# A two-layer-pair transformer on one core: GpSimd fill and mask work taken out of layer 0, ones rows written in small loads, a new planner model

## The chip, the cores and the metric

The kernel runs on one core of one Trainium2 chip. Its engines each work through an instruction list of their own: TensorE (PE) multiplies matrices, VectorE (DVE) and ScalarE (ACT) do elementwise work and empty PSUM, GpSimd (POOL) does small set-up work, and SyncE (SP) and ACT issue DMAs. The metric is the device time of one execution in microseconds. The kernel before took 397.16 us, the median of four runs (394.88 to 398.32 us).

## The reference

Four residual layers are run over 2048 tokens of width 448, in bfloat16: attention (A), gated MLP (B), A, B, with the same weights both times. A query sees eight keys, at distances 0, 2, ..., 14, inside its own head.

```python
def _A_ref(x, wqkv, wo):
    B, S, D = x.shape
    H = 16; Dh = D // H
    W, dil = 8, 2
    ...
    idx = pos[:, None] - off[None, :]
    mask = idx >= 0
    ...
    logits = jnp.einsum("bhsd,bhswd->bhsw", q, kg) * scale
    logits = jnp.where(mask[None, None, :, :], logits, -1e9)
    attn = _softmax(logits, axis=-1)
    o = jnp.einsum("bhsw,bhswd->bhsd", attn, vg)
    return (lambda x, *d: x.transpose(*d))(o, 0, 2, 1, 3).reshape(B, S, D) @ wo

def _B_ref(x, w_gate, w_up, w_down):
    g = jnp.einsum("bsd,df->bsf", x, w_gate)
    u = jnp.einsum("bsd,df->bsf", x, w_up)
    h = g * u
    return jnp.einsum("bsf,fd->bsd", h, w_down)

x = A_x
x = x + _A_ref(_layernorm(x, axis=-1), A_wqkv, A_wo)
x = x + _B_ref(_layernorm(x, axis=-1), B_w_gate, B_w_up, B_w_down)
x = x + _A_ref(_layernorm(x, axis=-1), A_wqkv, A_wo)
x = x + _B_ref(_layernorm(x, axis=-1), B_w_gate, B_w_up, B_w_down)
```

The inputs named `B_x` are not used by the result.

## The kernel before, in words

Even and odd tokens are kept apart (the first 1024 columns are the even ones), so that a dilated window becomes a plain window of eight neighbours. Layers are numbered 0 to 3: 0 and 2 are attention, 1 and 3 the MLP. Each layer is cut into chunks of 256 or 512 tokens; a job "A03" is chunk 3 of layer 0. `SEQ` (L70) lists the jobs in order, and layers overlap: B10 is already listed before A03.

An attention chunk does this. DVE and ACT make the layer norm of each block of 128 tokens (L614 to L635, the last writes `xn_sb`); the block is transposed, in layer 0 by PE through `ident` (L644) and copied from PSUM (L650), in the later layers by a DMA transpose (L638). PE projects Q and K (`qk_chunk`, matmuls at L682), ACT or DVE copies them to `qk` (L734). PE projects V (L682 also), copied to `v_sb` (L823). Attention goes by groups of two query blocks of 120 queries: the scores, 64 small matmuls with 28 rows each ("S", L843); the exponential on ACT into `E_sb` (L850); the band mask, a multiplication by `MK` (L860); the product with V, 64 small matmuls ("AV", L877); then a normalisation on ACT and DVE (L891 to L918) and the output projection (L698).

The last four heads' V is computed along with K and Q, as extra columns. It goes by DMA from `qk` to a scratch tensor `vt` in DRAM ("PW", L743), seven DMAs a chunk, and is read back by a DMA transpose ("VT", L754). `vt` also needs rows of ones, which give the softmax sum: GpSimd fills 16 partitions of 2048 elements (`big1`, L570), and two DMAs on SP write them to the scratch tensors of the two attention layers (L573). The first three query blocks of layer 0 have no such detour (`PLAIN`).

An MLP chunk does 14 units of 14 matmuls (gate and up, L964), a copy of the gate from PSUM on ACT (L970), a product on DVE into `hT` (L973), and the down projection (L698, the last two blocks at L985). `hT` also serves as staging space at the start, for the attention weights, for the mask's parts and for `big1`, so the first writes of L973 wait for the DMAs that read it (L972).

At the start SP issues the x loads, two of the four attention weight loads, then the others; ACT issues the other two weight loads (L501), loads its function table (L509) and issues the two gate loads later (L580). Weights are spread into `WQK` on ACT, DVE or POOL (L557, L565). PE runs 48 matmuls on zeros until real work comes (L548).

The order of all this is not written by hand. A planner (`Sched`) holds every operation with an estimated time, dependencies and a priority, and plays the engines forward: an engine that is free takes the ready operation with the lowest priority number. The resulting order of each engine is what is emitted; on the chip each engine keeps it and waits on semaphores. Estimates and priorities therefore change the order and nothing else. `PR` holds priority offsets by kind of operation, `JP` by job, `HEAD_P` of the first layer norms; `XL`, `STL`, `WVL`, `BL` are assumed landing times of loads; `HOLD_A`, `HOLD_BA`, `HOLD_BB` say how long PE leaves small-matmul work waiting before it turns to it (at once when `HOLD_N`, two, are ready); `A_CAP` and `B_CAP` say how many of the eight PSUM banks attention and MLP work may hold while the other wants some. An S operation takes four banks, a QK or AV operation two. An S or AV group costs PE, in the plan, what `S_EST` says:

```python
S_EST = 270.0
...
by_pool = hp == 1 and li == 0 and (end - 1) // 512 < POOL_MASK
sc.add(("dve", "pool") if by_pool else "dve", ins, {"dve": dve_est(2 * w, 2.0, 60.0 * len(ins)), "pool": 2.2 * 2 * w},
...
big1 = hT[0:4 * VT, 6:8, :, :].rearrange("p f s n -> p (f s n)")
sc.add("pool", one(lambda E: E.memset(big1, 1.0), "c_big1"), 1800, prio=-20)
for li in (0, 2):
    dst = vt_dram[li].rearrange("(t r) n -> t r n", r=32)[:, DH:32, :]
    plain_dma("sp", dst, big1, ("vones", li), f"d_one{li}", deps=["c_big1"], lat=3000.0, prio=-10)
```

Of the kernel before, what the change touches and what calls it, by code (L numbers as in the profile page):

```python
# [9 lines left out]
S = 2048  # L10
D = 448
H = 16
DH = 28
# [6 lines left out]
NQB = 17  # L20
EW = 4 * 128
NGR = 9
SCALE = DH ** -0.5
# [6 lines left out]
HEAD_LN = 5  # L30
HEAD_P = (-32.07, -27.33, -20.7, -18.17, -14.17)
HOLD_A = 1000.0
HOLD_BA = 2000.0
HOLD_BB = 4000.0
HOLD_N = 2
S_EST = 270.0
DPARTS = ((0, 7), (7, 14))
S_AFTER = 9
POOL_MASK = 1
POOL_WQK = True  # L40
VFIRST = False
VT = 4
NV2 = 6
NXN_ = 6
NO = 4
NE_ = 2
# [3 lines left out]
NBK = 8  # L50
PR = {'AV': -1.13, 'rstd': -5.13, 'bn': -0.38, 'N': -4.34, 'Gps': -1.22, 'Tps': 9.06, 'H': 3.83, 'S': -5.56, 'VT': -3.59, 'Ex': 3.61, 'G': 7.67, 'xn': -0.19, 'QK': 2.33, 'Ddps': -11.05, 'V': 10.89, 'x': -0.46, 'lnv': -20.66, 'Oc': -5.93, 'Oa': 1.35, 'R': -8.64, 'VVps': 0.18, 'Yps': 0.16, 'PW': 28.27, 'T': -2.43, 'mv': 0.81, 'Rs': -0.7, 'Rl': 4.01, 'QKps': -0.61, 'E': 0.37}
JP = {'A20': -35.49, 'B32': 2.91, 'B34': 8.11, 'A22': -3.18, 'B13': 0.51, 'A21': 3.14, 'B12': 0.41, 'A02': 0.27, 'A03': 0.46, 'B30': 0.78, 'B31': 0.62, 'B10': -17.75, 'B11': 0.16, 'A23': 11.17, 'A04': 3.65, 'B33': 3.74, 'A01': -0.38, 'B14': -0.22, 'A00': -8.79}
XL = (3000.0, 3000.0, 4500.0, 5000.0, 5500.0)
WVL = 5000.0
STL = (3300.0, 4300.0, 3500.0, 4600.0)
BL = (11000.0, 15000.0, 8000.0)
KP = ((0, 3), (3, 7))
KT = (13000.0, 13500.0)
WOL = 6000.0
PLAIN = 3  # L60
ACH = {0: (256, 512, 512, 512, 256), 2: (512, 512, 512, 512)}
BCH = {1: (256, 512, 512, 512, 256), 3: (256, 512, 512, 512, 256)}
WARM = 18
FILL = 30
SEED = 375
JITTER = 0
ATT_P = 0.44
A_CAP = 8
B_CAP = 8
# [27 lines left out]
def grp_qbs(g):  # L97
    return [0] if g == 0 else [2 * g - 1, 2 * g]

# [25 lines left out]
class Sched:  # L125
# [5 lines left out]
    TAIL = {"pe": 0.0, "act": 125.0, "dve": 85.0, "pool": 100.0, "sp": 0.0}  # L131
    SWITCH = 92.0

    def __init__(self):
# [75 lines left out]
    def schedule(self):  # L210
# [4 lines left out]
        order = {e: [] for e in self.ENGS}  # L215
        mode = None
        ndep, users = {}, {}
        pend = {e: [] for e in self.ENGS}
# [19 lines left out]
        while left:  # L238
            moved = False
            b_ready = any(o.acquire is not None and o.acquire.kind == 1 for o in pend["pe"])  # L240
            for e in self.ENGS:
# [64 lines left out]
                if e == "pe":  # L306
                    if mode is not None and op.mode != mode:
                        est += self.SWITCH
                    mode = op.mode
                op.start, op.end = now, now + est  # L310
                free[e] = op.end
# [111 lines left out]
def build(nc, A_x, A_wqkv, A_wo, B_w_gate, B_w_up, B_w_down, out):  # L423
# [28 lines left out]
    v2_sb = sb([128, NV2, 128], bf, "v2_sb")  # L452
    E_sb = sb([128, NE, 4, EW], bf, "E_sb")
    R_sb = sb([128, NR, EW], dt.float32, "R_sb")
# [20 lines left out]
    def one(fn, key=None):  # L475
        return [(fn, key)]
# [30 lines left out]
    for q in range(2, NCH):  # L507
        load_x(q)
    sc.add("act", one(act_table_load), 1300.0, prio=-58)  # L509

# [9 lines left out]
    sc.add("pool", one(lambda E: E.memset(v_sb[:].rearrange("p s (h e) -> p (s h) e", e=32)[:, :, DH:32], 1.0), "c_v"), 400, prio=-40)  # L520
    sc.add("pool", one(lambda E: E.memset(v2_sb[:, 0:PLAIN, :].rearrange("p s (h e) -> p (s h) e", e=32)[:, :, DH:32], 1.0), "c_v2"), 200, prio=-39)
    memset("pool", MT, 1.0, "i_mt", 300)
# [45 lines left out]
    WVR = [("wv", 0), ("wv", 1)]  # L568
    big1 = hT[0:4 * VT, 6:8, :, :].rearrange("p f s n -> p (f s n)")
    sc.add("pool", one(lambda E: E.memset(big1, 1.0), "c_big1"), 1800, prio=-20)  # L570
    for li in (0, 2):
        dst = vt_dram[li].rearrange("(t r) n -> t r n", r=32)[:, DH:32, :]
        plain_dma("sp", dst, big1, ("vones", li), f"d_one{li}", deps=["c_big1"], lat=3000.0, prio=-10)  # L573
    for j in range(4):
# [10 lines left out]

    rings = {n: [None] * k for n, k in (("xn", NXN), ("o", NO), ("v", NV), ("v2", NV2), ("e", NE), ("r", NR), ("g", NG))}
    rpos = {n: 0 for n in rings}
# [16 lines left out]
    def ln_chunk(li, j, prio):  # L604
# [17 lines left out]
        for B in blocks:  # L622
# [14 lines left out]
            if not by_pe:  # L637
                sc.add("sp", one(lambda E, slot=slot, c0=c0: E.dma_start_transpose(X[:, :, c0:c0 + 128], xn_sb[:, slot, 0:128 * nt]), ("T", li, B)),  # L638
                       1300.0, deps=[("xn", li, B)] + war, dma=f"d_t{li}_{j}", mode=0, lat=2400.0 if li == 0 else 1400.0 if par == 0 else 1900.0, prio=prio)
            else:  # L640
# [61 lines left out]
    def qk_chunk(li, j, prio):  # L702
# [37 lines left out]
        for b, w in [(b, w) for b in range(4) for w in range(2) if b + w < 4 and (li, j) != (0, 0)]:  # L740
            src = qk[32 * b + DH:32 * b + 32, w, :, c0:c1]
            dst = vt_dram[li].rearrange("(t w b r) n -> r w b t n", w=2, b=4, r=4)[:, w, b, :, c0:c1]
            sc.add("sp", one(lambda E, dst=dst, src=src: E.dma_start(dst, src), ("PW", li, j) if b == 3 else None), 550.0, deps=[("QK", li, j, c) for c in range(4)], dma=f"d_p{li}_{j}", mode=0, lat=3000.0 if li == 0 and j <= 2 else 2200.0, prio=prio - 0.2)  # L743

    vslot, v2slot = {}, {}

    def vt_load(li, qb, prio):
        if li == 0 and qb < PLAIN:
            return
        k0, nk, _, _ = qb_info(qb)  # L750
        slot, prev = ring("v2", ("AV", li, qb))
        v2slot[(li, qb)] = slot
        deps = [("PW", li, j) for j in chunks_of(li, k0, k0 + nk)] + [("vones", li), prev]
        sc.add("sp", one(lambda E: E.dma_start_transpose(v2_sb[:, slot, :], vt_dram[li][:, k0:k0 + 128]), ("VT", li, qb)), 1300.0, deps=deps, dma=f"d_v{qb}", mode=li, lat=2000.0 if li == 0 and k0 < 1024 else 1500.0, prio=prio)  # L754

    def v_group(li, qbs, prio):
# [14 lines left out]
        tdeps = [("T", li, B) for B in sorted(blocks)] + [p for _, p in slots if p is not None]  # L771
        plain = li == 0 and qbs[0] < PLAIN
        split = len(qbs) == 1
# [170 lines left out]
    def b_chunk(li, j, n_b, prio):  # L944
# [15 lines left out]
        for m in range(FC):  # L960
# [6 lines left out]
            for u in us[m:m + 1]:  # L967
                bk, fc = u["bk"], u["fc"]
                gs, prev = ring("g", ("H", li, j, fc))
                sc.add("act", one(lambda E, gs=gs, bk=bk: E.activation(g_sb[:, gs, 0:nt], ps[:, bk[0], 0:nt], ACT.Copy), ("G", li, j, fc)), act_est(nt),  # L970
                       deps=[("Gps", li, j, fc), prev], release=[(bk, 0)], prio=prio)
                war = hslot_users.get((hs, "prev"), WQKR + [("vones", 0), ("vones", 2)] + [f"c_mk{k}" for k in range(3)])  # L972
                sc.add("dve", one(lambda E, gs=gs, bk=bk, fc=fc: E.tensor_tensor(hT[:, fc, hs, 0:nt], g_sb[:, gs, 0:nt], ps[:, bk[1], 0:nt], ALU.mult), ("H", li, j, fc)), dve_est(nt),  # L973
                       deps=[("G", li, j, fc), ("Ups", li, j, fc)] + war, release=[(bk, 1)], prio=prio)
# [29 lines left out]
    def grps_of(li, j):  # L1004
        a, z = CH[li][j]
        return [g for g in range(NGR) if a < sum(qb_info(grp_qbs(g)[-1])[2:]) <= z]

    done = {}

    def a_chunk(li, j, prio):  # L1010
# [14 lines left out]

        for g in grps_of(li, j):
            qbs = grp_qbs(g)
            while len(qbs) == 2 and (rpos["v"] % NV) == NV - 1:
# [86 lines left out]
```

## Time and profile before

| | us |
|---|---|
| median of 4 runs | 397.16 |
| lowest, highest | 394.88, 398.32 |
| the profiled execution, its own time | 398.32 |
| its span, first to last instruction | 396.6 |
| DVE busy | 278.6 (70%) |
| ACT busy | 199.6 (50%) |
| POOL busy | 10.2 (3%) |

So 1.7 us of the profiled execution lie outside its span, and it is 1.2 us above the median. PE's row, and the rows by stretch, stand in the prediction. A busy PE row says that some matmul was in flight, not that PE streamed at its full rate: matmuls overlap, and their ends are modelled. DMA carries 22.71 MB; its rate is 271, 287 and 266 GB/s in the first three slices of 9.9 us and 77 GB/s in the fourth, and never over 125 GB/s after that. So nearly all loads fall into the first 35 us.

### The profile page before, as it was taken

The page shows a single profiled execution, that of the slowest core. Times are in us where ns is not written, and L with a number is a line of the kernel's source. Part 1 is how long each engine was busy: PE and PEld are TensorE (multiplying, and loading weights), DVE is VectorE, ACT ScalarE, POOL GpSimd, SP SyncE. Part 2 cuts the span into 40 slices and gives each one's busy share as a digit, 9 for nine tenths or more (in the row PEclk, how much of TensorE's full clock was granted, in tenths as well). Part 3 has the DMA queues.
Part 4 walks back from the last instruction along what each step waited for, and adds up shares of the span by engine and source line. Part 5 has one row for each costly group of instructions (what it writes and reads, how often), then busy time and mean ns, then how long its engine had stood idle before and what let it go on. Part 6 is the DMA issues. An engine that isn't in the chain of part 4 may idle for free.

```text
span 396.6 us, 13913 instructions
## 1 busy us (share of the span) xinstructions
PE 385.4 (97%) x6142; PEld 216.2 (55%) x6142; DVE 278.6 (70%) x604; ACT 199.6 (50%) x387; POOL 10.2 (3%) x38
## 2 busy tenths in 40 slices
PE   7997999999999999999999999899999999999996
PEld 6553568655445454545545667654545444544584
DVE  6994799988976948694679856795693867344152
ACT  5785896736723556344661454753661354043040
POOL 7200000000000000000000000000000000000000
PEclk9998999999999999999999999999999999999999
DMA  8993153524020410213020335107102120400000
GB/s 271 287 266 77 25 63 67 58 56 75 3 47 16 75 26 16 48 26 41 15 49 2 47 36 96 28 8 125 20 0 48 57 41 0 77 20 2 23 27 23
DMA packets 54107, 22.71 MB, mean 57 GB/s; under 512 B 44992, under 2 KB 53120, under 8 KB 54048
## 3 DMA queue, kind: packets, MB, share of 16 engines
q1 hardware_dynamic: 53136, 19.72, 25.6%
q10 hardware_dynamic: 912, 2.12, 2.1%
q8 instruction: 48, 0.79, 0.9%
q14 instruction: 11, 0.09, 0.1%
HBM read 8.54 MB, written 2.83 MB: 29 GB/s over the span
## 4 chain that ended last, share of the span: by engine, by line
PE 88%; DVE 6%; ACT 2%; issue 2%; DMA 1%; DVEq 0%
PE ps L964 41%; PE ps L698 24%; PE ps L682 15%; PE ps L877 2%; PE ps L843 2%; PE ps L985 1%; DVE st L614 1%; DVE xn_sb L635 1%; DVE x_sb L935 1%; DMA x_sb<-in_A_x_dram 1%; PE ps L644 1%; DVE E_sb L860 1%; ACT g_sb L970 1%; ACT qk L734 0%; DVE oT L918 0%
## 5 line engine op out<-in xcount | busy, mean ns | idle before, releaser
L964 PE MATMUL ps<-xnTb,WGU 64*128 64x512 bf16 (+1 forms) x1960 | 179.6, 333 | 0.7 <-ACT rstd L619 0.5
L964 PEld LDWEIGHTS ps<-xnTb,WGU 64*128 64x128 bf16 x1960 | 94.2, 94 | 72.5 <-DVE x_sb L935 0.7
L970 ACT ACTIVATE g_sb<-ps 128x512 bf16<-128x512 f32 (+1 forms) x140 | 71.3, 512 | 120.5 <-PE ps L964 119.2
L973 DVE TENSOR_TENSOR hT<-g_sb,ps 128x512 bf16<-128x512 bf16 (+1 forms) x140 | 78.7, 573 | 42.3 <-ACT g_sb L970 41.2
L698 PE MATMUL ps<-WD,hT 64*128 64x448 bf16 x840 | 83.3, 349 | 0.0
L698 PEld LDWEIGHTS ps<-WD,hT 64*128 64x128 bf16 x840 | 40.7, 94 | 37.5
L935 DVE TENSOR_TENSOR x_sb<-x_sb,ps 128x448 bf16<-128x448 bf16 x62 | 35.9, 612 | 30.4 <-PE ps L698 30.4
L682 PE MATMUL ps<-xnTa,WQK 64*128 64x512 bf16 (+1 forms) x504 | 54.5, 356 | 0.6 <-DVE qk L734 0.2
L850 ACT ACTIVATE E_sb<-ps 128x1024 bf16<-128x1024 f32 (+1 forms) x36 | 33.8, 983 | 16.0 <-PE ps L843 15.0
L614 DVE BATCH_NORM_STATS2 st<-x_sb 128x6 f32<-128x448 bf16 x64 | 37.3, 613 | 2.7 <-DMA x_sb<-in_A_x_dram 2.7
L682 PEld LDWEIGHTS ps<-xnTa,WQK 64*128 64x128 bf16 x504 | 24.0, 94 | 23.1 <-issue 0.9
L635 DVE TENSOR_SCALAR xn_sb<-x_sb,mv,rstd 128x512 bf16<-128x512 bf16 (+1 forms) x64 | 34.8, 592 | 1.2 <-ACT rstd L619 0.8
L734 ACT ACTIVATE qk<-ps 128x1024 bf16<-128x1024 f32 (+1 forms) x26 | 22.9, 894 | 14.8 <-PE ps L682 14.8
L698 PE MATMUL ps<-wo_g,oT 64*128 64x448 bf16 x256 | 29.4, 349 | 0.1
L860 DVE TENSOR_TENSOR E_sb<-E_sb,MK 128x1024 bf16<-128x1024 bf16 (+2 forms) x39 | 23.2, 611 | 6.3 <-ACT E_sb L850 6.2
L918 DVE TENSOR_TENSOR oT<-O_sb,R_sb 128x480 bf16<-128x480 f32 (+3 forms) x36 | 22.0, 623 | 4.1 <-ACT R_sb L907 3.8
L905 DVE STREAM_SHUFFLE R_sb<-O_sb 128x480 f32<-128x480 f32 (+1 forms) x34 | 22.5, 696 | 0.0
L682 PE MATMUL ps<-WV,xnTa 64*128 64x336 bf16 (+3 forms) x252 | 21.1, 299 | 0.3
L906 ACT ACTIVATE R_sb<-R_sb 128x480 f32<-128x480 f32 (+1 forms) x34 | 19.8, 601 | 1.9 <-DVE R_sb L905 1.9
L734 DVE CAST qk<-ps 128x1024 bf16<-128x1024 f32 x10 | 12.2, 1223 | 12.2 <-PE ps L682 12.2
L907 ACT ACTIVATE R_sb<-R_sb 128x480 f32<-128x480 f32 (+1 forms) x34 | 19.9, 600 | 0.3
L617 ACT ACTIVATE lnv<-mv,eps_sb 128x2 f32<-128x2 f32 (+1 forms) x33 | 9.4, 293 | 20.7 <-DVE mv L616 20.5
(50 smaller groups left out, 181.5 us busy)
## 6 DMA issues: line engine op xcount, KB each, us to landing
out_dram<-x_sb SPq DMA_DIRECT2D x15, 112.0 KB, 1.7
WD<-in_B_w_down_dram SPq DMA_DIRECT2D x2, 784.0 KB, 13.5
x_sb<-in_A_x_dram SPq DMA_DIRECT2D x3, 448.0 KB, 5.5
WGU<-in_B_w_gate_dram ACTq DMA_DIRECT2D x1, 896.0 KB, 18.1
WGU<-in_B_w_up_dram SPq DMA_DIRECT2D x1, 896.0 KB, 19.8
vt<-qk SPq DMA_DIRECT2D x49, 16.0 KB
WGU<-in_B_w_up_dram SPq DMA_DIRECT2D x1, 672.0 KB, 20.6
WGU<-in_B_w_gate_dram ACTq DMA_DIRECT2D x1, 672.0 KB, 10.9
```

What stands on the lines that cost most here:

```text
L614: sc.add("dve", one(lambda E, B=B: E.bn_stats(st6[:, B, :], x_sb[:, B, :]), ("bn", li, B)), 525.0, deps=[("x", li - 1, B)] + ([("xn", li - ...
L635: sc.add("dve", one(lambda E, B=B, dst=dst, src=src: E.tensor_scalar(dst, src, mv[:, B, 0:1], rstd[:, B:B + 1], ALU.subtract, ALU.mult), ( ...
L682: parts[0 if s < 3 else 1][1].append((lambda E, w=w, c=c, lo=lo, st=st, sp_=sp_: E.matmul(u["out"](w), u["lhs"](w, c, lo, lo + 64), u["rhs ...
L698: ins.append((lambda E, w=w, c=c, lo=lo, st=st, sp_=sp_: E.matmul(outs(w), lhs(w, c, lo), rhs(w, c, lo), start=st, stop=sp_), keys[w] if s ...
L734: return E.activation(dst, src, ACT.Copy) if hasattr(E, "activation") else E.tensor_copy(dst, src)
L850: return E.activation(E_sb[:, slot, 2 * hp:2 * hp + 2, 0:w], ps[:, b0:b0 + 2, 0:w], ACT.Exp, scale=SCALE)
L860: return E.tensor_tensor(e, e, m, ALU.mult)
L905: sc.add("dve", one(lambda E: E.stream_shuffle(R_sb[:, rs, 0:w], O_sb[:, os_, 0:w], [DH] * 32), ("Rs", li, qb)), dve_est(w) + 100.0, deps= ...
L935: sc.add("dve", one(lambda E: E.tensor_tensor(x_sb[:, B, :], x_sb[:, B, :], ps[:, bk[w], 0:D], ALU.add), ("x", li, B)), dve_est(D), deps=[ ...
L964: ins.append((lambda E, u=u, k=k, w=w: E.matmul(u["out"](w), WGU[64 * w:64 * w + 64, k, 128 * u["fc"]:128 * u["fc"] + 128], X[64 * w:64 * ...
L970: sc.add("act", one(lambda E, gs=gs, bk=bk: E.activation(g_sb[:, gs, 0:nt], ps[:, bk[0], 0:nt], ACT.Copy), ("G", li, j, fc)), act_est(nt), ...
L973: sc.add("dve", one(lambda E, gs=gs, bk=bk, fc=fc: E.tensor_tensor(hT[:, fc, hs, 0:nt], g_sb[:, gs, 0:nt], ps[:, bk[1], 0:nt], ALU.mult), ...
```

## The change

Three edits change what is issued.

- `big1`, its memset on GpSimd and its two DMAs are gone. The ones rows are now written by eight DMAs on SP, four rows of `vt` each; the source is `ones32`, four partitions of 128 ones, read 16 times over. The VT transposes wait for four of them in place of one, and the first writes to `hT` (L972) no longer wait for them.
- `POOL_MASK` goes from 1 to 0: no mask multiplication may go to GpSimd.
- The table load on ACT gets priority -61, ahead of the two weight loads at -60.

The memset of ones in `v2_sb` covers four blocks instead of three. The rest changes the plan: new priorities, holds and caps, other assumed landing times, other times for transposes and PW writes, and a charge on PE for groups of many instructions: a credit of 36 instructions that refills at one in 4.17 ns, a group of more than 40 instructions (a matmul counts two) costs at least 4.17 ns for each that the credit doesn't cover, and 130 ns more when it is over the credit by 40. `PAIRED` is true, and with it the grouping of query blocks and the buffers are those of before; `PAIR_PLAIN[True]` is 3, like `PLAIN`.

```diff
-HOLD_A = 1000.0
-HOLD_BA = 2000.0
-HOLD_BB = 4000.0
+HOLD_A = 4000.0
+HOLD_BA = 4000.0
+HOLD_BB = 500.0
...
-POOL_MASK = 1
+POOL_MASK = 0
...
-XL = (3000.0, 3000.0, 4500.0, 5000.0, 5500.0)
+XL = (2300.0, 2200.0, 4200.0, 5000.0, 5500.0)
...
-STL = (3300.0, 4300.0, 3500.0, 4600.0)
+STL = (2400.0, 2600.0, 2900.0, 2800.0)
...
-ATT_P = 0.44
-A_CAP = 8
+ATT_P = 1.82
+A_CAP = 4
...
+    FETCH = 4.17
+    CREDIT = 36.0
+    HICCUP = 130.0
...
+                    n = 2 * len(op.ins)
+                    credit = min(self.CREDIT, credit + (now - clast) / self.FETCH)
+                    if n > 40:
+                        est = max(est, (n - credit) * self.FETCH + (self.HICCUP if n > credit + 40 else 0.0))
+                    credit = max(0.0, credit + est / self.FETCH - n)
+                    clast = now + est
...
-    sc.add("act", one(act_table_load), 1300.0, prio=-58)
+    sc.add("act", one(act_table_load), 1300.0, prio=-61)
...
-    big1 = hT[0:4 * VT, 6:8, :, :].rearrange("p f s n -> p (f s n)")
-    sc.add("pool", one(lambda E: E.memset(big1, 1.0), "c_big1"), 1800, prio=-20)
-    for li in (0, 2):
-        dst = vt_dram[li].rearrange("(t r) n -> t r n", r=32)[:, DH:32, :]
-        plain_dma("sp", dst, big1, ("vones", li), f"d_one{li}", deps=["c_big1"], lat=3000.0, prio=-10)
+    for li, t in [(li, t) for li in (0, 2) for t in range(VT)]:
+        dst = vt_dram[li][32 * t + DH:32 * t + 32, :].rearrange("r (a n) -> r a n", n=128)
+        src = ones32[0:4, :].unsqueeze(1).to_broadcast([4, 16, 128])
+        plain_dma("sp", dst, src, ("vones", li, t), f"d_one{li}", deps=["c_ones"], lat=3000.0, prio=-10 - (li == 0))
...
-                       1300.0, deps=[("xn", li, B)] + war, dma=f"d_t{li}_{j}", mode=0, lat=2400.0 if li == 0 else 1400.0 if par == 0 else 1900.0, prio=prio)
+                       1380.0, deps=[("xn", li, B)] + war, dma=f"d_t{li}_{j}", mode=0, lat=2200.0 if par == 0 else 2900.0, prio=prio)
...
-        deps = [("PW", li, j) for j in chunks_of(li, k0, k0 + nk)] + [("vones", li), prev]
-        sc.add("sp", one(lambda E: E.dma_start_transpose(v2_sb[:, slot, :], vt_dram[li][:, k0:k0 + 128]), ("VT", li, qb)), 1300.0, deps=deps, dma=f"d_v{qb}", mode=li, lat=2000.0 if li == 0 and k0 < 1024 else 1500.0, prio=prio)
+        deps = [("PW", li, j) for j in chunks_of(li, k0, k0 + nk)] + [("vones", li, t) for t in range(VT)] + [prev]
+        sc.add("sp", one(lambda E: E.dma_start_transpose(v2_sb[:, slot, :], vt_dram[li][:, k0:k0 + 128]), ("VT", li, qb)), 1300.0, deps=deps, dma=f"d_v{qb}", mode=li, lat=2300.0 if li == 0 and k0 < 1024 else 1900.0, prio=prio)
...
-                war = hslot_users.get((hs, "prev"), WQKR + [("vones", 0), ("vones", 2)] + [f"c_mk{k}" for k in range(3)])
+                war = hslot_users.get((hs, "prev"), WQKR + [f"c_mk{k}" for k in range(3)])
```

Every number in `PR`, `JP` and `HEAD_P` is replaced too; the PW write is planned at 340 ns on SP instead of 550.

## The prediction

> **What bounds the kernel now.** I read the page's first parts, then busy time by stretch, then the list of waits of PE, then the chain of waits and the timeline at the places these name.
>
> ```profile
> PE 385.4 (97%) x6142; PEld 216.2 (55%) x6142; DVE 278.6 (70%) x604; ACT 199.6 (50%) x387; POOL 10.2 (3%) x38
> ...
> PEclk9998999999999999999999999999999999999999
> ...
> q8 instruction: 48, 0.79, 0.9%
> ```
>
> PE is the bound. One slice of the clock row is low, and 48 packets of 16 KB carried instructions. Busy time by stretch (PE, PEld, DVE, ACT, POOL, then granted clock, DMA share, GB/s) shows where PE is not full:
>
> ```profile
> 0.00:9.50 9.50, 7.45 (x56) 5.67 (x56) 5.79 (x16) 5.72 (x12) 7.81 (x31) 1.00 0.84 266
> 9.50:60.00 50.50, 46.61 (x1030) 26.93 (x1032) 41.23 (x106) 40.58 (x79) 2.35 (x7) 0.97 0.64 144
> 60.00:377.00 317.00, 315.04 (x4822) 170.25 (x4823) 223.13 (x467) 147.91 (x283) 0.00 (x0) 1.00 0.23 39
> 377.00:396.60 19.60, 16.27 (x240) 13.32 (x234) 8.44 (x19) 5.36 (x14) 0.00 (x0) 1.00 0.08 25
> ```
>
> Up to 9.5 us PE only warms up and transposes; then 50.5 - 46.6 = 3.9 us are idle in the stretch that has attention alone, 2.0 us in the long middle, 3.3 us at the end. The middle is full, so what is saved early or in PE's idle places comes off the end. PE's waits:
>
> ```profile
> PE ps L843 <- issue: 2.1, 1, 2.1
> PE ps L877 <- issue: 1.5, 2, 1.3
> PE ps L644 <- DVE xn_sb L635: 1.3, 2, 0.8
> ...
> PE ps L985 <- DVE hT L973: 0.9, 1, 0.9
> PE ps L964 <- ACT rstd L619: 0.5, 1, 0.5
> ```
>
> The largest wait for nothing that the profile shows; the third is DVE's. The chain of waits has the first one between two halves of one S group, and a second inside a pair of AV groups:
>
> ```profile
> 32.16 0.54 PE ps L843 x52
> 32.69 2.15 issue
> 34.84 0.32 PE ps L843 x10
> ```
>
> ```profile
> 248.06 1.16 PE ps L877 x123
> 249.22 1.33 issue
> 250.55 0.21 PE ps L877 x5
> ```
>
> The records of the instruction queue show a 16 KB fetch starting at 32.12 and at 247.76, as these groups start, lasting 1.33 and 1.22 us. I read both gaps as PE running out of instructions: 64 matmuls with their weight loads are 128 instructions in some 0.54 us. After the first gap the clock is granted at half from 34.8 to 38.2 us.
>
> **The GpSimd memset and mask.** The timeline of DVE and of GpSimd:
>
> ```profile
> 5.95 1.93 POOL L570 MEMSET hT<- 16x2048 bf16 x1
> ```
>
> ```profile
> 7.19 1.16 DVE L635 TENSOR_SCALAR xn_sb<-x_sb,mv,rstd 128x512 bf16<-128x512 bf16 x2
> ```
>
> ```profile
> 16.91 1.27 POOL L860 TENSOR_TENSOR E_sb<-E_sb,MK 128x576 bf16<-128x576 bf16 x1 [2.91 <-ACT E_sb L850]
> ```
>
> ```profile
> 16.85 2.45 DVE L635 TENSOR_SCALAR xn_sb<-x_sb,mv,rstd 128x512 bf16<-128x512 bf16 x4
> ```
>
> Single records of L635 with 512 elements take 0.39 to 0.41 us. The one under the memset took 0.84, the one under the mask 1.48: both ended about when GpSimd did. Without the memset, 0.84 - 0.39 = 0.45 us go. The chain of waits runs through that instruction (7.19, 0.85 us) to the transposes, the copy and the first QK matmul at 9.51; the last WQK copy is on DVE behind it (8.27 to 8.66) and moves too. Bounds: 0 to -0.45 (a later x or weight landing takes its place); I take -0.45. At 16.9, 1.48 - 0.40 = 1.08 us go, and the mask comes to DVE at 0.44 (L860 at 16.49): -0.64 on DVE, in front of a transpose for which PE idled 0.53. Bounds +0.44 (where no L635 was delayed) to -0.64; I take -0.5, PE's idle time. Sum: **-0.95**.
>
> **The ones rows.** SP's timeline:
>
> ```profile
> 15.45 1.46 SPq L483 DMA_DIRECT2D vt<-hT  x2
> 25.33 2.48 SPq L743 DMA_DIRECT2D vt<-qk  x7
> 35.59 2.31 SPq L754 DMA_TRANSPOSE v_sb<-vt  x1
> ```
>
> Eight issues at the 0.31 us median of L743 are 2.5 us in place of 1.46. Behind them on SP stand the PW writes of A01, which wait for QK until 25.33: 1.0 us more ends at 18, so 0. On the DMA engines, 512 pieces of 256 bytes at 21.5 ns (the 256-byte packets of 47 to 52 us) are 11 us, over 16 engines 0.7 us, instead of 32 of 4 KB at about 0.27 us (3,584-byte packets took 0.235), 0.5 us. The first VT starts at 35.59, when the PW writes behind the weights have landed; its data are in at 39.0 and the next query block's at 40.3, and the AV group that needs them starts at 45.5. With 5 us of cover it costs 0; without cover 0.2. The Trainium skill ("DMA: Bandwidth & Descriptors", Specifications) speaks against this edit: below 512 bytes a transfer is a read-modify-write. An estimate by that rule, each piece twice, is 1.4 us, still inside the cover.
>
> **The table load.** ACT's timeline:
>
> ```profile
> 0.83 0.91 ACTq L483 DMA_DIRECT2D hT<-in_A_wqkv_dram  x2
> 1.76 1.28 ACT L480 ACT_TABLE_LOAD   x1 [1.76 <-PEq L1100]
> ```
>
> ACT's first work is at 4.28, behind the weights; a load done at 2.1 instead of 3.04 helps nobody. What counts is whether the two weight DMAs then go out 1.28 us later. In the trace ACT's sequencer ran its next wait at 1.80, under the load, and at 13.78 issued a DMA while ACT computed. So I take 0. If they are held: the WQK copies end up to 1.28 later against a slack of 9.51 - 8.66 = 0.85, +0.4; but x (4.2 us to landing beside these 448 KB) comes sooner, at most by about as much as they are held, and DVE's start with it: -0.8 after the same slack. Bounds +0.4 to -0.8.
>
> **The plan.** This is the large term and the uncertain one. 32 of the S and AV groups are full ones; from first matmul to the next operation they take 0.64 us (192.40 to 193.04), where the plan has 0.27 + 0.09 for the switch; with the new charge 0.51 to 0.66 + 0.09. So the plan gets some 32 x 0.27 = 8.6 us of PE time that it did not know, and pays for back-to-back pairs. Nothing shows the new order, so I price the places that an order can avoid. The gap at 32.69: 2.15, plus the half clock (eight matmuls 1.82 instead of 0.97, and some 0.4 on what follows), 1.25: 3.4. The gap at 249.22: 1.33, and 0.5 in another AV pair at 196.2 (1.70 against 2 x 0.6): 1.8. The wait of 0.47 at 59.46, before the first MLP unit, whose transposes landed at 59.6; the plan gave them 1300 + 1900 ns from issue to landing (now 1380 + 2900), and they take 3.0 us in the median and 4.8 at most. Together 5.7, and I take all of it as gone: the two gaps are meetings of a fetch with a small-matmul group, the new charge acts on such groups, and the transposes are now planned longer. Lower bound of the gain 0 (the fetches come every 256 instructions in any order and meet other groups); beyond that the order can lose, see below. A rule of the Trainium skill weighs against this ("Runtime: NRT & Kernel Launch", Instruction fetch mechanics): the sequencer fetches the next 16 KB while it runs the current one and the crossing is mostly hidden. By it the charge buys little and the sum would end near 397. The two gaps above are not hidden, and I go by them.
>
> **Sum.** -0.95 + 0 + 0 - 5.7 = -6.65 on the profiled 398.32: **391.7 us**. The profiled run is 1.2 above the median, so against 397.16 this is -1.4%.
>
> **The rivals.**
>
> *The stalls only move.* Another order meets as many fetches. For it: 48 fetches and 36 groups, and half clock after any long gap. Against: the page shows only two long gaps, both in small groups. Then only -0.95 is left: 397.4.
>
> *Attention is starved (slower).* `A_CAP` 4 lets an S group start, while MLP work is ready, only when attention holds no bank at all, and the holds for attention go to 4 us. If layer 2's attention then lags behind the end of layer 1's MLP, it runs alone, as in 9.5 to 60 us, where 3.9 of 50.5 us (7.7%) are idle against 0.6% in the middle. Three of layer 2's four chunks alone are about 60 us: 0.07 x 60 = +4.3. It decides when more than one chunk of layer 2 is still to do as layer 1's units end. Against: while MLP work is ready PE is full. With the stalls moved too: 397.4 + 4.3 = 401.7.
>
> *More than priced.* The new order also halves the idle time that is left in the first stretch and at the end (3.9 + 3.3 less the 2.15 + 0.5 + 0.47 counted above, 4.1): -2.0, 389.7.
>
> *The edits do not do what they say.* The remaining GpSimd copies (12.92 to 13.99, L564) could block DVE as the mask did; then the 0.95 goes as well, 398.3. It counts with the first rival.
>
> **How the numbers follow.** 1% is 4.0 us, about what a measurement of this kernel can tell from no change; the four runs span 3.4. Forecast 0.42 (own range 388 to 394.5: 0.34 faster, 0.08 same); more than priced 0.14 (faster); stalls move 0.25 (395 to 399: 0.04 faster, 0.19 same, 0.02 slower); starved 0.19 (399 to 405: 0.03 same, 0.16 slower). Faster 0.52, same 0.30, slower 0.18. Beside their middle values the cases have a spread of 3 to 4 us, that of the four runs. The range leaves out a third of the fastest case, half of the starved one and a little of the others: 386 to 401.
>
> **What would show it.** Records of L635 with 512 elements all near 0.40 us and the first QK matmul near 9.0: the GpSimd term. No PE wait for "issue" over 1 us and no half clock after 5 us: the plan term; gaps of 1 to 2 us inside L843 or L877 elsewhere: the first rival. ACT's weight loads issued before 1.0 us: the table load is free; after 2.0: it holds them. A stretch of tens of us between 100 and 300 without L964: the starved case. The forecast is wrong if idle time of PE after 9.5 us stays above 8 us, or if matmuls run slow without idling.

## The result, and the profile after

The changed kernel takes 397.25 us, the median of 35 executions (394.71 to 400.27); the kernel before takes 396.6 beside it (56 executions, 394.88 to 402.17). The ratio is 1.0009, 95% interval [0.9994, 1.0024]. A gain of 1.4% was forecast and there is none. The profiled execution took 396.95 us, with a span of 395.1. Line numbers move by 13 or 14: L644 is now L657, L682 L695, L743 L756, L754 L767, L843 L856, L877 L890, L964 L977.

The rows of the page for engines, clock and instruction queue:

```profile
PE 384.0 (97%) x6142; PEld 215.0 (54%) x6142; DVE 277.8 (70%) x606; ACT 200.2 (51%) x385; POOL 7.2 (2%) x37
...
PEclk9999899999999999999999999999999999999999
...
q8 instruction: 48, 0.79, 0.9%
```

One slice is still low, and it has moved from the fourth to the fifth. Busy time by stretch, in the columns used before (the last row reaches past the end of the span, 395.1, so 1.5 us of it are empty):

```profile
0.00:9.50 9.50, 7.45 (x59) 5.78 (x61) 5.71 (x18) 4.42 (x10) 5.95 (x30) 1.00 0.83 269
9.50:60.00 50.50, 45.19 (x964) 26.39 (x960) 41.55 (x107) 38.04 (x71) 1.25 (x7) 0.97 0.60 141
60.00:377.00 317.00, 316.58 (x4952) 172.43 (x4948) 224.62 (x471) 154.73 (x298) 0.00 (x0) 1.00 0.23 40
377.00:396.60 19.60, 14.79 (x182) 10.40 (x176) 5.94 (x14) 3.02 (x8) 0.00 (x0) 1.00 0.08 25
```

PE's idle time in the middle fell from 2.0 to 0.4 us, as hoped. In the stretch of attention alone it rose from 3.9 to 50.50 - 45.19 = 5.3. What was won late was lost early. PE's list of waits says on what:

```profile
PE ps L890 <- DMA v_sb<-vt: 2.9, 1, 2.9
PE ps L657 <- issue: 1.5, 1, 1.5
...
PE ps L657 <- DVE xn_sb L648: 0.9, 1, 0.9
PE ps L856 <- issue: 0.5, 1, 0.5
```

The largest wait is new: an AV group waits for a VT transpose, the transfer that the prediction gave 5 us of cover. SP's timeline between 14 and 45 us shows why it is late:

```profile
14.57 16.52 SPq L497 DMA_DIRECT2D vt<-ones  x8
31.22 3.33 SPq L756 DMA_DIRECT2D vt<-qk  x7
36.82 4.73 SPq L767 DMA_TRANSPOSE v_sb<-vt  x3
```

The eight ones loads hold SP for 16.5 us (single issues 0.79, 0.67, 0.63, 3.68, 6.69, 1.53, 1.60 and 0.63 us). Behind them the PW writes go out at 31.22 in place of 25.33. The chain of waits follows it to PE:

```profile
33.97 2.84 DMA vt<-qk
36.81 0.02 issue
36.82 1.20 SPq L767
38.02 0.04 issue
38.07 3.33 DMA v_sb<-vt
41.40 0.14 issue
41.53 0.74 PE ps L890 x60
```

PE was idle from 38.66 to 41.53, and as the idle time ended the granted clock fell to half, from 41.49 to 44.90. Busy time by stretch around it (clock is the third figure from the end):

```profile
38.60:41.50 2.90, 0.07 (x2) 0.00 (x0) 2.02 (x3) 1.76 (x2) 0.00 (x0) 1.00 0.10 12
41.50:44.90 3.40, 3.27 (x82) 1.84 (x84) 1.42 (x3) 2.22 (x4) 0.00 (x0) 0.50 0.19 31
```

This half-clock window decides how the times are to be read. One window of 3.4 us at half rate makes a mean clock of 1 - 1.7/395 = 0.996 over an execution, two 0.991, so the mean clock of each execution tells how many it had. Of 29 executions of before on one chip, 21 had none (mean 395.73 us) and 8 one (397.98): an execution with a window is some 2.2 us longer, the stall that brought the window included. Of the 36 entries of after in the list of clocks (one more than in the list of times), 1 had none (394.71), 24 one (mean 396.99), 11 two (398.30). The profiled execution of before, from which the prediction's sum was made, was one of the rarer ones with a window.

### The profile page after: what moved, and what is told of

It reads as the page before. It is cut to its first block, busy times and chain, and to the rows that moved or that the text cites. A ratio compares the mean times of both kernels' runs of the same rounds, so it can differ in the third digit from the quotient of the medians.

```text
span 395.1 us, 13933 instructions
## 1 busy us (share of the span) xinstructions
PE 384.0 (97%) x6142; PEld 215.0 (54%) x6142; DVE 277.8 (70%) x606; ACT 200.2 (51%) x385; POOL 7.2 (2%) x37
## 4 chain that ended last, share of the span: by engine, by line
PE 94%; DMA 3%; SPq 1%; DVE 1%; issue 0%; ACT 0%; DVEq 0%
PE ps L977 43%; PE ps L711 27%; PE ps L695 17%; PE ps L890 3%; PE ps L856 2%; PE ps L998 1%; DMA x_sb<-in_A_x_dram 1%; PE ps L657 1%; DMA v_sb<-vt 1%; DMA vt<-qk 1%; SPq L756 1%; DVE st L627 0%; SPq L767 0%; PE ps L562 0%; ACT qk L747 0%
## 5 line engine op out<-in xcount | busy, mean ns | idle before, releaser
L977 PE MATMUL ps<-xnTb,WGU 64*128 64x512 bf16 (+1 forms) x1960 | 178.2, 333 | 0.1
L977 PEld LDWEIGHTS ps<-xnTb,WGU 64*128 64x128 bf16 x1960 | 94.2, 94 | 71.8 <-issue 0.2
L711 PE MATMUL ps<-WD,hT 64*128 64x448 bf16 x840 | 84.4, 349 | 0.0
L695 PE MATMUL ps<-xnTa,WQK 64*128 64x512 bf16 (+1 forms) x504 | 52.1, 353 | 0.2
L747 ACT ACTIVATE qk<-ps 128x1024 bf16<-128x1024 f32 (+1 forms) x24 | 21.8, 916 | 32.2 <-PE ps L695 32.2
L695 PEld LDWEIGHTS ps<-xnTa,WQK 64*128 64x128 bf16 x504 | 23.8, 94 | 23.1 <-PE ps L695 0.7
L648 DVE TENSOR_SCALAR xn_sb<-x_sb,mv,rstd 128x512 bf16<-128x512 bf16 (+1 forms) x64 | 33.7, 568 | 1.2 <-ACT rstd L632 1.2
L873 DVE TENSOR_TENSOR E_sb<-E_sb,MK 128x1024 bf16<-128x1024 bf16 (+2 forms) x40 | 24.0, 608 | 12.0 <-ACT E_sb L863 12.0
L747 DVE CAST qk<-ps 128x1024 bf16<-128x1024 f32 (+1 forms) x12 | 13.5, 1132 | 15.0 <-PE ps L695 15.0
L695 PE MATMUL ps<-WV,xnTa 64*128 64x336 bf16 (+3 forms) x252 | 22.9, 308 | 0.3
```

Source lines behind the costliest of these rows:

```text
L648: sc.add("dve", one(lambda E, B=B, dst=dst, src=src: E.tensor_scalar(dst, src, mv[:, B, 0:1], rstd[:, B:B + 1], ALU.subtract, ALU.mult), ( ...
L695: parts[0 if s < 3 else 1][1].append((lambda E, w=w, c=c, lo=lo, st=st, sp_=sp_: E.matmul(u["out"](w), u["lhs"](w, c, lo, lo + 64), u["rhs ...
L711: ins.append((lambda E, w=w, c=c, lo=lo, st=st, sp_=sp_: E.matmul(outs(w), lhs(w, c, lo), rhs(w, c, lo), start=st, stop=sp_), keys[w] if s ...
L747: return E.activation(dst, src, ACT.Copy) if hasattr(E, "activation") else E.tensor_copy(dst, src)
L873: return E.tensor_tensor(e, e, m, ALU.mult)
L977: ins.append((lambda E, u=u, k=k, w=w: E.matmul(u["out"](w), WGU[64 * w:64 * w + 64, k, 128 * u["fc"]:128 * u["fc"] + 128], X[64 * w:64 * ...
```

## The experiments

The theory after the first look: the new order is better by some 3 us, and the small ones loads give it back by holding SP, that is, by keeping SP busy with their issue while other DMAs wait behind them. Rivals: the order itself is no better, or it puts the AV group too early whatever the loads are; or the number of DMAs (eight for two) holds SP, not their pieces. All variants keep the order of the kernel they start from, but for the two that change the planner and for the operations that a code cut shows moved, added or left out. Ratios are to the kernel before, timed beside each variant; the variants ran on several chips, on which before itself took 395.56 to 396.52 us.

**Two loads with large pieces** (16 pieces of 4 KB each), in the order of after; GpSimd fills `big1` early.

```diff
+    cop.ins = [(cop.ins[0][0], None), (lambda E: E.memset(big1, 1.0), "c_ones")]
...
+        keep.ins = [(lambda E, li=li: E.dma_start(vt_dram[li].rearrange("(t r) n -> t r n", r=32)[:, DH:32, :], big1), ("vones", li, 0))]
```

> The changed kernel with every engine's order kept, but the ones rows again in two loads of 16 pieces of 4 KB from a region filled by GpSimd, here early (behind the small ones tile, about 2.3 us, where no norm runs). Theory (SP held by the eight small loads): they are issued within 2 us of 14.6, the first L756 writes go out at 25 to 26 instead of 31.2, the first L767 transpose near 35.5 instead of 36.8, the AV group at 41.5 starts 1.3 to 2.9 earlier, and PE's wait of 2.87 for it shrinks to 1.6 or less; with the half clock gone too the time is 2 to 4.5 us below the changed kernel's, 393 to 395.5. Rival (the weights that still land until 34 set the transposes, whoever issues): the writes go out early but land no sooner than 36, and the time is that of the changed kernel, 397 +- 1.

393.04 us (12 executions), ratio to before 0.9939 [0.9912, 0.9965]. The loads hold SP for 1.45 us, the PW writes go out at 25.39, and no PE wait for VT is left.

**Two loads with small pieces** (256 pieces of 256 bytes each), in the order of after.

```diff
+        keep.ins = [(lambda E, li=li: E.dma_start(vt_dram[li].rearrange("(t r) (a n) -> t r a n", r=32, n=128)[:, DH:32], ones32[0:4 * VT, :].unsqueeze(1).to_broadcast([4 * VT, 16, 128])), ("vones", li, 0))]
```

> The changed kernel, order kept, with the same 512 pieces of 256 bytes from the ones tile, but in two loads of 256 pieces instead of eight of 64. If the number of pieces holds SP: the two issues take together about as long as the eight (16.5 us, to about 31), and the time is the changed kernel's, 397. If the number of loads holds SP: both are out by 17 and the time is that of the two large loads, 393 to 395.5.

396.2 us, 1.0008 [0.9978, 1.0037]. SP's timeline:

```profile
14.84 3.09 SPq L1070 DMA_DIRECT2D vt<-ones  x2
25.15 8.27 SPq L756 DMA_DIRECT2D vt<-qk  x7
35.64 4.63 SPq L767 DMA_TRANSPOSE v_sb<-vt  x3
```

The two loads themselves pass in 3.1 us, not the 16.5 that I had expected if the pieces were at fault, but the next DMA, the first PW write, is held: 5.56 of the 8.27 us are its issue alone. VT starts at 35.64 and PE waits 2.8 us for it. Two DMAs are enough, so it is not the number of DMAs.

**Eight loads with large pieces** (four pieces of 4 KB each), in the order of after.

```diff
+            sc.ready[("vones", li, t)][0].ins = [(lambda E, li=li, t=t: E.dma_start(vt_dram[li][32 * t + DH:32 * t + 32, :], big1[4 * t:4 * t + 4, :]), ("vones", li, t))]
```

> The changed kernel, order kept, with eight loads of 4 pieces of 4 KB from the region that GpSimd fills early. If the number of pieces holds SP: eight issues of some 0.4 to 0.7 us, out by 20, and the time is 393 to 395.5. If the number of loads holds it: SP is held until about 31 as in the changed kernel, and the time is 397.

393.11 us (12 executions), 0.9917 [0.9891, 0.9943]: with the two large loads (0.9939), faster than both kernels of the case. SP's timeline and busy time by stretch:

```profile
14.81 3.18 SPq L1074 DMA_DIRECT2D vt<-hT  x8
25.19 2.38 SPq L756 DMA_DIRECT2D vt<-qk  x7
33.36 4.05 SPq L767 DMA_TRANSPOSE v_sb<-vt  x3
```

```profile
9.50:60.00 50.50, 48.67 (x1088) 29.43 (x1090) 46.07 (x117) 42.18 (x81) 1.25 (x7) 1.00 0.58 146
60.00:377.00 317.00, 316.87 (x4912) 195.11 (x4908) 222.61 (x467) 152.76 (x294) 0.00 (x0) 1.00 0.23 39
```

The prediction's price of an issue, 0.31 us, holds for these (0.29 to 0.51), and the PW writes wait for QK and not for SP. PE idles 1.8 us in the early stretch (5.3 in after) and 0.1 in the middle. Same order, same number of DMAs, same bytes; the pieces differ, and some 3 to 4 us with them: 397.25 against 393.11, not timed side by side, and 396.20 against 393.04 for the two loads of each kind, timed on one chip. The small pieces are also read from a tile that is repeated 16 times, the large ones from a filled region; size and repetition were not separated.

The records of the DMA packets show when the pieces themselves moved. The 32 large ones went at 28.9 to 31.1 us, the 512 small ones of after at 29.2 to 32.9: in both kernels behind nearly all of the weights (packets of 3,584 bytes, until 30.5 and 32.2). The large pieces waited there with SP free again at 18.0; with the small ones SP was held until 31.1. The pieces are no load on the DMA engines: the 512 took 9.9 us in sum, the 32 took 5.2.

**Small loads, issued earlier**: the eight loads of after stand ahead of the WD and the later WGU loads on SP.

```diff
+    at = o.index(sc.ready[("wd", 0)][0])
+    o[at:at] = vo
```

> The changed kernel, order kept on all engines but SP, where the eight small loads stand ahead of the MLP weight loads (from about 9.7 us). Theory (they are held because the weight loads before them fill SP's queue): they take 0.4 to 0.7 us each and are out by about 15; the weight loads go out 3 to 5 us later, which nobody waits for before 60 us; the writes of L756 go out at 25 to 26, and the time is 393 to 395.5. Rival (the weights' landing sets the transposes): the weights land later by as much, the transposes move from 36.8 to 38 or later, and the time is 397 to 399.

400.91 us (6 executions), 1.0131 [1.0094, 1.0168], beyond both of my ranges and the worst place of all. SP's timeline:

```profile
9.74 5.99 SPq L497 DMA_DIRECT2D vt<-ones  x8
15.78 1.84 SPq L497 DMA_DIRECT2D WD<-in_B_w_down_dram  x2
17.66 6.62 SPq L497 DMA_DIRECT2D WGU<-in_B_w_up_dram  x2
```

The ones loads now pass at 0.64 to 0.85 us each; the two WGU loads behind them take 6.62 us to issue, against 3.84 in the run above. VT goes out only at 41.85, PE waits 2.0 us for it, and the gaps put down to "issue" grow to 3.2 and 1.7; why they grow is open.

**Small loads in the old order**: the kernel before with eight small loads, the memset and the mask left as they were.

```diff
+        op.ins = [(lambda E, li=li, t=t: E.dma_start(vt_dram[li][32 * t + DH:32 * t + 32, :].rearrange("r (a n) -> r a n", n=128), ones32[0:4, :].unsqueeze(1).to_broadcast([4, 16, 128])), None) for t in range(VT)]
```

> The kernel before, order kept, with the ones rows in the eight loads of 64 pieces of 256 bytes (the memset on GpSimd stays). Theory: SP is held to about 31 us, the transposes into v_sb move from 35.6 to near 37 and their data from 39.0 and 40.3 to 41 and 42.5, but in this order the AV group that needs them starts at 45.5, so the time moves by no more than 0.5 us, 396 to 396.5. Rival (the pieces cost also by themselves, on the DMA engines or by later weights): +2 us or more, 398 or more.

398.72 us (12 executions), 1.0031 [1.0, 1.0061]: not the 396 to 396.5 that I had expected. SP is held here too, for 15.04 us from 14.47, and VT starts at 37.68 in place of 35.59. No AV group waits: the old order has the one that needs VT at 45.30. So the cover that the prediction counted existed, but in the old order. 0.7 us were lost all the same in executions without a half-clock window (396.52, four of them, against 395.78), and 8 of 12 had a window, against 11 of 30 of before beside it; why is open. In the profiled execution the window, 11.01 to 14.43, began before the first ones load was issued. It came 1.6 us after a wait of PE of 2.01 us, for the first norm. There the memset, which this kernel keeps, ran at the same time as another instruction of DVE than in the profile of before. From the timelines of GpSimd and of DVE:

```profile
5.95 1.79 POOL L570 MEMSET hT<- 16x2048 bf16 x1
```

```profile
6.06 1.82 DVE L556 COPY WQK<-hT 128x448 bf16<-128x448 bf16 x1
```

Without the memset beside it the same copy takes 0.26 us. It stands ahead of the first norms, and the first QK matmul came at 10.79. Here x had come 0.2 us later than in the profile of before, and so this copy lay under the memset and not a norm.

**The charge alone**: the kernel before, planned with the charge on groups of many instructions.

```diff
+                    n = 2 * len(op.ins)
+                    credit = min(self.CREDIT, credit + (now - clast) / self.FETCH)
+                    if n > 40:
+                        est = max(est, (n - credit) * self.FETCH + (self.HICCUP if n > credit + 40 else 0.0))
```

> The kernel before with one thing of the change: the planner's charge for groups of many instructions (and the new order that comes of it). By the prediction's plan term: gaps over 1 us for issue vanish and the time is 2 to 4 us lower, 392 to 394. By the rival that stalls only move: gaps of 0.5 to 2 us for issue appear at the same counts of PE instructions as in the other kernels (about 690, 945 and so on, 256 apart), and the time is anywhere between 394 and 400.

400.92 us (5 executions, none with a half-clock window), 1.0087 [1.0054, 1.0121]: slower, and beyond both of my ranges. Gaps over 1 us for "issue" did not vanish: one of 1.50 us stands at 39.78, among the Q and K projections (L692), one projection matmul behind an S and an AV group.

**The new numbers without the charge**: the kernel with eight large loads, planned with the charge switched off.

```diff
-                    if n > 40:
+                    if n > 4000:
```

> The kernel after_eight_big, planned with the new priorities, holds, caps and landing times and without the charge on groups of many instructions; another order, the same instructions. If the new numbers carry the gain of the order (the charge alone made the order of before slower by 0.9%), it stays within 1 us of after_eight_big, 392.5 to 394. If the charge and the numbers were chosen together and an order gains only as a whole, it takes 396 or more.

409.95 us (4 executions), 1.0337 [1.0291, 1.0383]: far slower, the second of the two cases. None of its gaps for "issue" is over 0.8 us, so these do not explain its time. PE's waits:

```profile
PE ps L711 <- DVE hT L986: 3.9, 3, 2.3
PE ps L977 <- DVE hT L986: 2.5, 4, 1.0
PE ps L977 <- ACT E_sb L863: 2.0, 4, 1.1
PE ps L977 <- ACT g_sb L983: 1.8, 2, 1.7
```

These are waits for MLP products, exponentials and copies from PSUM; waits of this size for them stand in neither list of before or after. Neither the charge nor the new numbers carry the gain alone; the two together do. Which feature of the order makes it better was not isolated.

**Where "issue" comes from.** I counted PE's records, matmuls and weight loads, ahead of each such gap. In before the early one stands at 945; in after two stand at 693 and 949, which are 256 apart; with large pieces at 949 again. Orders differ, the count nearly doesn't (some records can be missing). The late one of before, at 8547, has partners at 8547 to 8550 in five other profiles. But a count only says where a gap can be: in the order of before, two further profiles (the small loads, and the first one under the GpSimd term) run through the same place without one. Two runs shift the count by small matmuls on zeros ahead of the warm-up, 40 and then 80 of one column, 80 and 160 instructions; the extra matmuls compute nothing that is used.

```diff
+    wop.ins = [(lambda E: E.matmul(ps[:, wb[0], 0:1], warm[:, 0:128], warm[:, 0:1], start=True, stop=True), None)] * 40 + wop.ins
```

> The kernel with eight loads of 4 KB pieces, with 40 matmuls of one column put ahead of the first warm-up matmul on PE, where PE has nothing to do. They add 80 PE instructions, so that every later instruction comes 80 counts later. Theory (PE runs out of instructions at the end of a 256-instruction block): no gap for issue at the transposes near 31 us; the block's end, at count 945 to 949, now falls into a run of projections, where PE is slow enough, and the gap of 0.76 us goes without a new one over 0.3 us before 60 us; the time is 0 to 1 us lower, 392 to 393. Rival (the gap belongs to the transposes or to what they wait for): it stays at L657 near 31 us with 0.7 us or more.

395.73 us (12 executions), 0.9982 [0.995, 1.0014], some 2.6 above the unshifted kernel. PE's timeline:

```profile
30.33 0.32 PE L856 MATMUL ps<-qk 28*64 28x64 bf16 x28
32.46 0.47 PE L856 MATMUL ps<-qk 28*64 28x64 bf16 x36 [1.82 <-issue]
```

I had expected the count to fall among projections, and it fell into the S group just ahead of the transposes. The gap left the transposes for that S group, stayed at 949, and grew from 0.8 to 1.8 us. So it belongs to the count and not to the transposes.

> The kernel after_eight_big with 80 one-column matmuls on zeros added ahead of the warm-up matmuls, so that every later instruction of PE has a place in the list 160 further on. Theory of the instruction blocks: gaps of PE that are put down to issue stand at the counts of before, 693, 949, 1205 and so on; at 949 PE is now among the Q and K projections (wide matmuls that run for long per instruction), so no gap over 0.4 us between 26 and 34 us; no gap at 31 us in the transposes or in the S group, where the variants with shifts of 0 and 80 instructions had theirs. The 80 small matmuls run while PE waits for the first x anyway, so they cost 0 to 0.3 us, and the time is 392.5 to 393.5, that of after_eight_big. Rival, the gap belongs to the place in the work and not to the count: a gap of 0.7 to 1.8 us at 30 to 32 us stays, in transposes or S, and the time is 394 to 396.

394.55 us (12 executions), 0.9977 [0.9948, 1.0007]. With 160 instructions the count lies among the projections (29.64 us), and no wait for "issue" is left in PE's list; all five unshifted profiles in this order have one at 949. The time did not follow. The small matmuls took 2.29 us at the start and the fills behind them ended later, so the first QK matmul came at 10.98 in place of 9.42; I had priced that at 0 to 0.3. VT went out 1.9 us later with it, and PE waited for it:

```profile
PE ps L890 <- DMA v_sb<-vt: 2.5, 1, 2.5
PE ps L1073 <- DVE eps_sb L526: 1.1, 1, 1.1
PE ps L695 <- DMA xnTa<-xn_sb: 0.3, 1, 0.3
```

The place of the gap is explained by the count; that removing it saves time is not shown.

**The GpSimd term** was tried in the order of before: the memset early and the mask on DVE.

```diff
+    sc.order["pool"].insert(sc.order["pool"].index(cop) + 1, mop)
...
+        op.eng = "dve"
```

> The kernel before with its order kept, but the memset of the ones region moved ahead on GpSimd (behind the small ones tile, about 2.3 us), and the one mask that went to GpSimd done by DVE right after the other half's mask. Theory (the prediction's term of 0.95 us): all records of L635 with 512 elements at 0.39 to 0.41 us, the first QK matmul near 9.05 instead of 9.51, and the time 0.5 to 1.0 us below the kernel before, 395.0 to 395.5. Rival (DVE's lost time was covered): the records are short, but the time stays within 0.3 us of before.

396.59 us, 1.0005 [0.9976, 1.0034]. The first norms are short (445 and 404 ns), but the first QK matmul came at 10.04, later than before. PE's timeline shows what stood in the way, 42 filling matmuls, which in this execution ran until 8.79 (the clock rose to full at 7.12 us, in the profile of before at 4.06):

```profile
3.66 5.14 PE L548 MATMUL ps<-hT 128*128 128x256 bf16 x30
8.63 0.39 PE L644 MATMUL ps<-ident,xn_sb 128*128 128x128 bf16 x4
```

Two more runs take eight of them away from there, first to a place behind the second transposes, then altogether.

```diff
+    for o in ahead:
+        pe.remove(o)
+    at = pe.index(t1_) + 1
+    pe[at:at] = ahead
```

> The order of before with the early fill of ones and the mask on VectorE, as in before_no_pool, and besides eight of the 42 filling matmuls on zeros stand behind the second group of transposes instead of ahead of the first. Nothing of the computation changes. If the delayed first norm is worth something and the filling matmuls swallowed it in before_no_pool, the first QK matmul starts 0.5 to 0.9 us sooner than the 10.04 of that run, near 9.1, and the time is 0.5 to 0.9 below that of the kernel before, taken over executions without a half-clock window. If the term does not exist (the x or weight landing, or what follows it, sets the time), the first QK matmul may move and the time stays within 0.3 of the kernel before.

395.76 us, 0.9993 [0.9966, 1.002]. The first QK matmul came at 9.61, now held by the 13 fills behind the transposes (8.09 to 9.68), so it does not test the start of the projections. Without a half-clock window 394.92 (8 executions) stand against 395.26 (17) of before, and in the run ahead of it 396.10 (8) against 395.78 (19): a third of a us in either direction.

> As before_no_pool (the order of before, the ones filled early, the mask on VectorE), with eight of the 42 filling matmuls on zeros left out, none put elsewhere. In before_no_pool the 42 fills ran until 8.79 and the first QK matmul came at 10.04; with eight moved behind the second transposes they still stood ahead of the first QK matmul, which came at 9.61. Without them the transposes are bound by the first norm alone. If the delayed first norm was worth its 0.45 us, the first QK matmul starts at 8.9 to 9.1 against 9.51 in the profile of before, and the executions without a half-clock window lie 0.4 to 0.9 below those of before. If the second WQK copy or a later x sets the start of the stretch that follows, the first QK matmul moves and the time stays within 0.2.

The first QK matmul came at 8.94, 0.57 us sooner than in before. The time did not: 397.37 us, 1.0026 [0.999, 1.0061]. Without a half-clock window 395.26 (4 executions, 394.08 to 396.90) stand against 395.52 (13) of before; 8 of 12 executions had a window or more, 4 of 17 of before. PE's timeline of one of the 8:

```profile
31.17 0.68 PE L843 MATMUL ps<-qk 28*64 28x64 bf16 x61
34.31 0.26 PE L843 MATMUL ps<-qk 28*64 28x64 bf16 x3 [2.46 <-issue]
```

In before the same S group is cut behind 52 matmuls, here behind 61. Eight matmuls, 16 instructions, less ahead of it, and the cut comes that much later in the work, at a count of 947: the shift experiment once more, unasked.

## Why the prediction was wrong

**The step that failed is the ones rows: "With 5 us of cover it costs 0".** It has two errors. The issues were priced at "the 0.31 us median of L743", taken from DMAs of 16 pieces of 1 KB; with 512 pieces of 256 bytes behind the weight loads they took 16.5 us in place of 2.5. Large pieces in the same places took 3.2 and small ones in two DMAs held the next DMA by 5.56, so it is the pieces. And the cover was read from the old order, where the AV group starts at 45.5; the new order has it at 38.7. The term was not 0 but +3 to +4: 3.2 between small and large pieces in two loads on one chip, 4.1 between 396.99 (after, one window) and 392.90 (large pieces, no window), which were not timed side by side. The wait itself is 2.9 and an execution with a window is 2.2 longer; how the two share the 3 to 4 was not separated.

The rule of the Trainium skill that the prediction weighed here ("DMA: Bandwidth & Descriptors", Specifications, read-modify-write below 512 bytes) gave an estimate of 1.4 us on the DMA engines. The packets do not show it: the 512 pieces of after took 9.9 us in sum, by estimate 0.6 if spread over 16 engines, about the 0.7 that the prediction took from the packets. What was measured was a hold of the engine that issues.

**The plan term, -5.7, was right in three of its places and too large for the median.** The gap at 249, the loss in the AV pair at 196 and the wait at 59.46 are gone from the profile of after; behind 100 us a single wait of 0.2 us is left. The first gap came back at its count, in other work (1.54 us in after, 0.76 with eight large loads). That gap with its half clock, 3.4 of the 5.7, was taken from an execution of a rarer kind: 21 of 29 executions of before have no window, and its 2.2 us can't be saved where they are not paid. Between profiled spans the order with large pieces saves 396.6 - 390.4 = 6.2 us; between executions without a window 395.73 - 392.90 = 2.8. The reason given, "the new charge acts on such groups", is not borne out: the order that the charge makes by itself is 0.9% slower and has a gap of 1.5 us, and that of the new numbers without it is 3.4% slower with no gap over 0.8 us. One sum of the prediction was off besides: "4.1" of idle time left takes off the 0.5 at 196, which lies in the long middle; at the start and the end 4.6 were left. Only the middle value of "more than priced" rests on it.

**The GpSimd term, -0.95: the norms became short, and no gain was measured.** In the changed kernel all ten norms take 396 to 415 ns, where two took 841 and 1482:

```profile
L648 DVE TENSOR_SCALAR xn_sb<-x_sb,mv,rstd x10: 396/407/415, 7.2 to 18.1; 128x512 bf16<-128x512 bf16 x10
```

Yet the first QK matmul moved only from 9.51 to 9.38 (fills on zeros kept PE until 9.45), and where it moved by 0.57, no gain was measured. The four executions that say so lie 2.8 us apart, so that the term itself could hide in the scatter; in the two runs with eight each, the difference is 0.3 one way and 0.3 the other. The term's size was also that of one execution: what the memset holds up depends on when x lands, 0.45 us of a norm in one profile, 1.6 of a copy in another, where PE waited 2.0 us and a window followed. How much the median execution paid for it is open.

**The table load, 0, was right.** ACT's timeline:

```profile
0.81 1.28 ACT L494 ACT_TABLE_LOAD   x1 [0.81 <-PEq L1114]
0.85 0.95 ACTq L497 DMA_DIRECT2D hT<-in_A_wqkv_dram  x2
```

The weight loads go out under the table load, at 0.85 (0.83 before).

**The rivals.** The number of "the stalls only move" (397.4) came out, mostly by luck: the gap of instructions did return at its count, 1.54 us at 31.22, but most of the loss was a stall that no rival named, and with large pieces the same order takes 393. The prediction set its own mark, PE idle after 9.5 us above 8: it is 5.3 + 0.4 + 3.3 = 9.0. Behind 62 us the longest stretch without L977 is 16.9 us (13.1 in before), and PE idled 0.4 us in the whole middle, so the starved case did not occur.

## What to carry to other kernels

Price a DMA issue from a row with the same size of pieces and the same traffic ahead of it, and look at what waits behind it on its queue: a load that nobody needs soon can still hold the one that somebody does. Where a change reorders the work, a cover read from the old order is no cover. Before a stall of one profile is counted as a gain, see from the clocks of the other executions how many of them have it.

## What the runs showed of the hardware

- **Small pieces hold the issuing queue while large loads are under way.** 512 pieces of 256 bytes in eight loads behind the weights held SP for 15.0 to 16.5 us; as 32 pieces of 4 KB, 1.45 to 3.2. The hold falls on whatever stands behind: the later ones loads, the PW write, or the weights. Either kind of piece moved only at 28 to 35 us, behind the weights; only the small ones kept SP waiting for that. Which resource ran full was not tested.
- **PE's instruction gaps sit at fixed counts.** The early ones stood at 693 and at 945 to 949 records in two orders, with five kinds of loads, and after shifts of 80 instructions one way and 16 the other. Not every execution has them: in the order of before three of five profiles have the one at 945 to 947. They ended 1.3 to 1.6 us after a 16 KB fetch had ended. The Trainium skill ("Runtime: NRT & Kernel Launch", Instruction fetch mechanics) gives blocks of 256 instructions, which agrees with 949 - 693 = 256, and calls the crossing mostly hidden; where it meets small matmuls or transposes, or comes a few wide matmuls behind them, the runs show up to 3.2 us; in the one run that put it deep into projections, nothing.
- **A stall shorter than a window can bring a whole half-clock window.** 2.9 us of idle PE were followed by 3.4 us at 0.50. In the profiles at hand each of the eight idle times of 2.0 us and more behind the warm-up was followed by a window; of the nine of 1.5 to 2.0 us three were (1.50, 1.73 and 1.82) and six were not. The Trainium skill ("TensorE: Matmul & The Clock Gate", Part 1) gives the window as 3413 ns, which agrees, and lets the clock fall after at least one idle window; here 2.9 us were enough.
